# Causal attention with soft expert slots: the upper half of k moved by a transfer within SBUF, the cast of q moved to the pair's second round, and two mask products per score tile in place of three

## The chip, the cores and the metric

The kernel runs on one core of one Trainium2 chip. The metric is the device time of one execution in microseconds (us). Engines are named as the profile names them: PE is the matrix engine (TensorE), PEld its loads of stationary weights, DVE the vector engine, ACT the scalar engine, POOL GpSimd, SP the engine that issues most transfers.

## The reference

The work is causal attention for 8 batches of 12 heads (sequence 448, head size 64), followed by a soft mixture of experts over the attention's output.

```python
scores = scale * np.matmul(q, k.transpose(0, 1, 3, 2))
scores = np.where(mask, -1000000000.0, scores)      # mask: strictly upper triangle
scores = scores - np.max(scores, axis=-1, keepdims=True)
attn = np.exp(scores)
attn = attn / (np.sum(attn, axis=-1, keepdims=True) + 1e-09)
attn_out = np.matmul(attn, v)                       # then x: (3584, 768)
logits = x @ phi                                    # 32 slots, 8 experts
slot_input = softmax(logits, axis=0).T @ x
slot_out[e] = relu(slot_input[e] @ w1[e]) @ w2[e]
out = softmax(logits, axis=1) @ slot_out
```

Everything is float32 from outside.

## The kernel before

**Attention.** Heads go in pairs (`NPAIR` = 48), a pair is loaded together, and each head has one round of the main loop (`for i in range(NHD + 1)`, line 480). Rounds with even `i` (the pair's first head) follow `ORDER[0]`, odd ones `ORDER[1]` (lines 42 to 47). Each tuple is written out by hand and names steps in the order in which every engine gets them; `_InOrder` keeps that order on each engine. Inside round `i` three heads are in work: the first score pass of head `i+2`, the second pass and the exponential of head `i`, and the product with v of head `i-1`.

**Score tile.** A head's causal scores, transposed (keys on partitions), lie in one PSUM tile of 1024 columns (two banks of 512, three such tiles). The four key chunks of 128 start at columns `SCOL` = (512, 0, 320, 960): chunk 0 with its 448 queries and chunk 3 with its 64 fill one bank, chunks 1 and 2 the other. The first pass, `scores1` (line 211), is named `c0`, `c3`, `c12` (mask products: identity in bf16 as weights, the triangle tile `tri` streamed, 128, 64 and 2 x 128 columns) and `k0` to `k3` (weights: a chunk of the rounded k, `ks`; streamed: the rounded q, `qd`; 448, 320, 192 and 64 columns). The second pass, `scores2` (line 285, `t0` to `t3`), adds what rounding left over and the row maximum, with weights `k2` and streamed tile `r2`.

**Operands.** For pair `p`, ACT casts k (`ck`, line 191) and q (`cq`, line 187) to the rounded type. POOL subtracts to get the remainders (`sk`, line 195; `sq`, line 205). ACT copies the rounded k from partitions 0 to 63 of `ks` to partitions 64 to 127 of `k2` (`c2`, `copy_k2`, line 200). Each of these tiles has two buffers, chosen by `p % 2`. In before, `ck` and `cq` of pair `p+2` are both in the even round, `c2` of pair `p+1` at the end of the odd round.

**Row maximum.** ACT evacuates chunk 0's scores (`ev`), DVE takes maxima over the chunks, transposes and reduces (`x0` to `x4`), PE transposes (`mr0`), DVE reduces (`mr1`), POOL spreads the result into `r2` (`sp`). `exp` (ACT) reads the whole score tile, and only after it is that tile free for another head. `a0` to `a3` are the products with v, `n0` to `n2` the normalization. `plan` (line 407) adds, in some rounds, transposes of the result, logits and dispatch; its pattern repeats every 12 rounds.

**Loads.** SP issues all loads: per pair k, v and q, and a tile of expert weights every other pair (22 during attention). A program order on SP, as on the other engines, is the order of the text: the loads stand at the start of odd rounds.

**Start and end.** Scores of heads 0 to 3 are computed ahead of, or in, the first two rounds by `scores1_all`; the steps of these rounds that start with `c`+digit, `k` or `t` and the steps `ev` and `exp` are skipped there. After the attention come the last logits, the experts and the combination, with the remaining expert weights streamed from HBM.

Of the kernel before, what the change touches and what calls it, by code (L numbers as in the profile page):

```python
# [9 lines left out]
F32 = mybir.dt.float32  # L10
F32R = mybir.dt.float32r
BF16 = mybir.dt.bfloat16
AF = mybir.ActivationFunctionType
ALU = mybir.AluOpType
# [3 lines left out]
P = 128  # L18
NB, NH, S, HD = 8, 12, 448, 64
# [10 lines left out]
NEG = -float(2 ** 33)  # L30
NHD = 2 * NPAIR
NR, XB = 2, 3
# [7 lines left out]


ORDER = (
# [4 lines left out]
)  # L47

SC0, SC1, SC2, SC3 = 512, 0, 320, 960
CQ0 = (0, 128, 256, 384)  # L50
SCOL = (SC0, SC1, SC2, SC3)

# [27 lines left out]
def attention_soft_moe(ctx: ExitStack, tc: tile.TileContext, qk, va, phi, w1, w2, out):  # L80
    nc = _Core(tc)
    const = ctx.enter_context(tc.tile_pool(name="const", bufs=1, side="left"))
# [29 lines left out]
    def load_qk(p, a, hs=slice(0, 2)):  # L112
        if p < NPAIR:
            if hs.start == 0:

                st["raw", a, p] = (wres.tile([P, WN], F32, tag="w", name=f"qk{a}_{p}")[:, 0:2 * S]
                                   .rearrange("p (h s) -> p h s", h=2)
                                   if (p, a) in ((1, 0), (2, 1)) else
                                   raw.tile([P, 2, S], F32, tag="qk", name=f"qk{a}_{p}"))
            nc.sync.dma_start(out=st["raw", a, p][:, hs], in_=qk[p, :, a, hs])  # L120

    def loads_v(p, eng=nc.sync):
        if p < NPAIR:
            eng.dma_start(out=va_[p % 2], in_=va[p])
# [12 lines left out]
    def load_w(n):  # L137
        if n < len(order):
            m, e, h, u = order[n]
            t = wtiles[order[n]] = slot(n, f"w{n}")  # L140
            nc.sync.dma_start(out=t, in_=(w1 if m == 0 else w2)[e, h, :, WN * u:WN * u + WN])

    for hs in (slice(0, 1), slice(1, 2)):
# [10 lines left out]
    nc.gpsimd.memset(ident, 0.0)  # L154
    nc.gpsimd.affine_select(out=ident, in_=ident, compare_op=ALU.not_equal, fill=1.0,
                            base=0, pattern=[[-1, P]], channel_multiplier=1)
    tri = const.tile([P, P], BF16, name="tri")
    nc.gpsimd.memset(tri, 0.0)
    nc.gpsimd.affine_select(out=tri, in_=tri, compare_op=ALU.is_ge, fill=NEG,
                            base=0, pattern=[[1, P]], channel_multiplier=-1)  # L160

    ops = [[fix.tile([P, 2, S], F32R, name=f"{o}{i}") for o in ("qd", "ks")] for i in range(NR)]
    qd_, ks_ = ([t[k] for t in ops] for k in range(2))
    ops = [[fix.tile([P, 2, S], F32R, name=f"{o}{i}") for o in ("k2", "r2")] for i in range(NR)]
    k2_, r2_ = ([t[k] for t in ops] for k in range(2))
# [33 lines left out]

    def copy_k2(p, hs=slice(0, 2)):  # L200
        if p < NPAIR:
            nc.scalar.activation(out=k2_[p % NR][64:P, hs], in_=ks_[p % NR][0:64, hs],
                                 func=AF.Copy)

    def sub_q(p, hs=slice(0, 2), eng=None):
        if p < NPAIR:
# [4 lines left out]
    def scores1(i, part):  # L211
        if i >= NHD:
            return
        p, h = divmod(i, 2)
        ks, qd = ks_[p % NR], qd_[p % NR]
        if ("s", i) not in st:
            st["s", i] = ps_s.tile([P, 1024], F32, tag="s", name=f"s{i}")
            st["open"] = set()
        s = st["s", i]

        bank = part in ("c12", "k1", "k2")
        start = bank not in st["open"]
        st["open"].add(bank)
        if part[0] == "k":
            c = int(part[1])
            w, m = S - CQ0[c], min(P, S - P * c)
            nc.tensor.matmul(s[0:m, SCOL[c]:SCOL[c] + w], ks[:, h, P * c:P * c + m],
                             qd[:, h, CQ0[c]:S], start=start, stop=False, skip_group_check=True)
            return
        if part == "c12":  # L230
            o = s[:, SC1:SC1 + 2 * SC2].rearrange("p (a n) -> p a n", n=SC2)[:, :, 0:P]
            mask = tri.unsqueeze(1).to_broadcast([P, 2, P])
        else:
            w = P if part == "c0" else S - 3 * P
            o, mask = s[:, SCOL[int(part[1])]:SCOL[int(part[1])] + w], tri[:, 0:w]
        nc.tensor.matmul(o, identb, mask, start=start, stop=False, skip_group_check=True)

    def scores1_all(i):
        for part in ("c0", "k3", "c3", "c12", "k2", "k1", "k0"):
            scores1(i, part)  # L240

    def max_evac(i):
# [42 lines left out]
    def scores2(i, cs):  # L285
        if i >= NHD:
            return
        p, h = divmod(i, 2)
        s = st["s", i]
        k2, r2 = k2_[p % NR], r2_[p % NR]  # L290
        for c in cs:
            w, m = S - CQ0[c], min(P, S - P * c)
            nc.tensor.matmul(s[0:m, SCOL[c]:SCOL[c] + w], k2[:, h, P * c:P * c + m],
                             r2[:, h, CQ0[c]:S], start=False, stop=True, skip_group_check=True)
# [5 lines left out]
    def attv(i, qcs, first):  # L300
        if not 0 <= i < NHD:
            return
        p, h = divmod(i, 2)
        pt, v, po = pt_[i % 2], va_[p % 2], st.get(("po", i), po0)
        for qc in qcs:
            for c in range(qc + 1):
                col = SCOL[c] + P * (qc - c)


                m = P if qc < 3 or i == NHD - 1 and c < 3 else 65  # L310
                nc.tensor.matmul(po[0:m, qc], pt[:, col:col + m], v[:, c, h],
                                 start=c == 0 and qc in first, stop=c == qc, skip_group_check=True)

# [93 lines left out]
    plan = {}  # L407
    for b in range(NB):
        o, last = 12 * b, b == NB - 1
# [14 lines left out]
    for hs in (h0, h1):  # L424
        cast_k(0, hs)
        cast_q(0, hs)
        sub_k(0, hs, nc.vector)
        sub_q(0, hs)
    scores1_all(0)
    scores1_all(1)  # L430
    warm(START[1])
# [48 lines left out]
    for i in range(NHD + 1):  # L480
        p, h = divmod(i, 2)
        if h:
            load_qk(p + 3, 1)
            if p + 1 < NPAIR - 1:
                loads_v(p + 1)
            load_qk(p + 3, 0)
            if p % 2 and nload < RES:
                load_w(nload)
                nload += 1
        if i == NHD - 3:  # L490

            loads_v(NPAIR - 1, nc.scalar)
        if i < 2:
            scores2(i, (1, 0, 2))
            if i:
                scores1_all(3)
                max_evac(3)
            scores2(i, (3,))
            exps(i)
            if i == 0:  # L500
                max_row(1, 0)
                max_row(1, 1)
                max_spread(1)
                sub_q(1, h1)

        qs = [int(n[1]) for n in ORDER[h] if n[0] == "a"]
        first = qs[:2] if qs[0] == 3 else qs[:1]
        for n in ORDER[h]:
            if i < 2 and (n in ("ev", "exp") or n[0] in "kt" or n in ("c0", "c3", "c12")):
                continue  # L510
            if i == 0 and n in ("mr0", "mr1", "sp"):
                continue
            if n[0] == "k" or n in ("c0", "c3", "c12"):
                scores1(i + 2, n)
            elif n[0] == "t":
                scores2(i, (int(n[1]),))
            elif n[0] == "a":
                attv(i - 1, (int(n[1]),), first)
            elif n[0] == "x":
                max_keys(i + 2, int(n[1]))  # L520
            elif n[0] == "n":
                norm(i - 1, int(n[1]))
            elif n in ("mr0", "mr1"):
                max_row(i + 1, int(n[2]))
            elif n == "ld":
                if i % 12 == 3 and i > 12:
                    logits_d(i // 12 - 1, lt)
            elif n == "plan":
                if later and i:
                    later.pop(0)()  # L530
                plan.get(i, int)()
            else:
                {"ev": lambda: max_evac(i + 2), "exp": lambda: exps(i), "sp": lambda: max_spread(i + 1),
                 "ck": lambda: cast_k(p + 2), "sk": lambda: sub_k(p + 2), "cq": lambda: cast_q(p + 2),
                 "c2": lambda: copy_k2(p + 1), "sq": lambda: sub_q(p + 2)}[n]()
        if i == NHD - 1:

            scs.close()
            pe = att.enter_context(tc.tile_pool(name="pe", bufs=1, space=PSUM, reuse_waits="tile"))
            ps = [pe.tile([P, 512], F32, name=f"e{k}") for k in range(6)]  # L540
            po = st["po", i] = ps[2][:, 0:NCH * VC].rearrange("p (c n) -> p c n", n=VC)
# [44 lines left out]
    for hf in range(2):  # L586
        tps = (po0 if hf == 0 else po).rearrange("p a b->p (a b)")[:, 0:3 * NSLOT]
        for c in range(3):
            o = 384 * hf + P * c
# [130 lines left out]
    n = NBUF  # L720
# [80 lines left out]
```

## Time and profile before

| what | value |
|---|---|
| three runs | 461.1, 459.82, 461.09 us (median 461.09) |
| profiled execution: time / span of its instructions | 459.88 us / 458.2 us |
| busy share of the span: PE, PEld, DVE, ACT, POOL | 93%, 79%, 76%, 72%, 58% |
| mean granted PE clock | 0.978 |
| bytes moved, mean rate | 119.04 MB, 260 GB/s |

All instructions of the kernel body are recorded under one line (line 64, the `_InOrder` helper), so groups are told apart by the tiles that they write and read: `s<-tri,identb` is a mask product, `s<-qd,ks` a first-pass product, `s<-r,k` a second-pass one, `po<-va,pt` the product with v. In this kernel a float32 product (`po`) takes two instructions. A matmul's start is a record, its end is modelled; rows of the timeline that show "x10" cover ten instructions, from the first start to the last end. "128*64 128x192" means weights of 128 rows by 64 columns and 192 streamed columns.

### The profile page before, as it was taken

How to read it: one execution, taken by the hardware profiler on the slowest of the kernel's cores; microseconds unless marked ns; L12 is line 12 of the kernel's file. 1: busy time of each engine (PE TensorE's matmuls, PEld its weight loads, DVE VectorE, ACT ScalarE, POOL GpSimd, SP SyncE). 2: the span in 40 equal slices, each digit the busy share in tenths (PEclk: the TensorE clock that was granted, in tenths of full speed). 3: DMA queues.
4: the chain of work that ended last, by engine and by line, in shares of the span. 5: the costliest groups of instructions: out<-in, count | busy, mean ns of one | idle time of the engine just before them, and what ended most of it. 6: DMA issues, size and time to landing. Idle time of an engine off the chain costs nothing.

```text
span 458.2 us, 12014 instructions
## 1 busy us (share of the span) xinstructions
PE 424.9 (93%) x4581; PEld 362.3 (79%) x4581; DVE 348.9 (76%) x1044; ACT 329.9 (72%) x496; POOL 266.3 (58%) x215
## 2 busy tenths in 40 slices
PE   6899999999999999999999999999999998996660
PEld 3798999999899989998999999999989654542230
DVE  6988888888888898888888888888886467332350
ACT  6898899889888988897899789988975211342240
POOL 5888777777777777777778777777771000000000
PEclk9999999999999999999999999999999999999875
DMA  7477666676667765777666766667758999999997
GB/s 267 128 259 243 235 193 224 216 239 223 204 208 237 236 221 171 241 241 231 210 188 225 254 222 216 191 213 253 231 160 300 369 411 415 414 414 413 402 391 284
DMA packets 38201, 119.04 MB, mean 260 GB/s; under 512 B 4096, under 2 KB 11776, under 8 KB 38144
## 3 DMA queue, kind: packets, MB, share of 16 engines
q1 hardware_dynamic: 38000, 118.01, 75.6%
q8 instruction: 36, 0.59, 0.5%
q10 hardware_dynamic: 144, 0.27, 0.2%
q14 instruction: 21, 0.17, 0.1%
HBM read 107.25 MB, written 11.01 MB: 258 GB/s over the span
## 4 chain that ended last, share of the span: by engine, by line
PE 77%; DMA 11%; POOL 5%; ACT 1%; DVE 1%; issue 1%; SPq 0%; POOLq 0%; ACTq 0%
PE po L64 34%; PE s L64 24%; DMA w<-in_w_dram 10%; PE xt L64 4%; PE g L64 3%; PE hp L64 3%; POOL r L64 3%; PE sp L64 2%; PE rt L64 2%; PE pp L64 2%; POOL ks L64 1%; PE e L64 1%; PE so L64 1%; DMA qk<-in_qk_dram 1%; ACT ot L64 0%
## 5 line engine op out<-in xcount | busy, mean ns | idle before, releaser
L64 PE MATMUL po<-va,pt 128*128 128x65 f32 x1900 | 193.6, 250 | 0.1
L64 PEld LDWEIGHTS po<-va,pt 128*128 128x128 f32 x1900 | 190.5, 171 | 0.5 <-issue 0.3
L64 DVE TENSOR_TENSOR mx<-s,mx 128x320 f32<-128x320 f32 (+2 forms) x288 | 100.8, 350 | 31.4 <-ACT mx L64 27.9
L64 POOL TENSOR_TENSOR r<-qk,qd 64x896 fp32r<-64x896 f32 (+1 forms) x50 | 101.5, 2030 | 6.5 <-ACT qd L64 2.7
L64 POOL TENSOR_SCALAR_AFFINE_SELECT r<-mr 14x448 fp32r<-14x448 f32 x96 | 61.4, 640 | 73.2 <-DVE mr L64 72.8
L64 ACT ACTIVATE pt<-s 128x1024 f32<-128x1024 f32 x96 | 98.2, 1023 | 6.3 <-PE s L64 3.1
L64 POOL TENSOR_TENSOR ks<-qk,ks 64x896 fp32r<-64x896 f32 (+1 forms) x47 | 98.1, 2087 | 4.5 <-ACT ks L64 0.9
L64 PE MATMUL s<-r,k 128*128 128x320 f32 (+3 forms) x384 | 83.2, 298 | 2.3 <-POOL r L64 2.2
L64 ACT ACTIVATE mx<-s 128x448 f32<-128x448 f32 x96 | 52.5, 546 | 36.0 <-PE s L64 22.2
L64 PE MATMUL s<-qd,ks 128*128 128x448 f32 (+3 forms) x384 | 76.0, 308 | 1.6 <-ACT qd L64 1.6
L64 PEld LDWEIGHTS s<-r,k 128*128 128x128 f32 (+1 forms) x384 | 60.0, 176 | 6.4 <-POOL r L64 2.9
L64 DVE STREAM_TRANSPOSE mt<-mx 128x448 f32<-128x448 f32 x96 | 61.9, 645 | 3.3
L64 DVE TENSOR_REDUCE r<-mt 128x14 f32<-128x448 f32 x96 | 58.4, 609 | 0.1
L64 PEld LDWEIGHTS s<-qd,ks 128*128 128x128 f32 (+1 forms) x384 | 55.0, 180 | 3.1 <-ACT qd L64 2.3
L64 ACT ACTIVATE ks<-qk 128x896 fp32r<-128x896 f32 (+1 forms) x50 | 45.6, 914 | 2.5 <-DMA qk<-in_qk_dram 2.5
L64 ACT ACTIVATE k<-ks 64x896 fp32r<-64x896 f32 (+1 forms) x49 | 45.8, 935 | 1.1
L64 ACT ACTIVATE qd<-qk 128x896 fp32r<-128x896 f32 (+1 forms) x50 | 46.1, 923 | 0.4 <-DMA qk<-in_qk_dram 0.3
L64 PEld LDWEIGHTS <-identb 128*128 128x128 bf16 x320 | 28.1, 99 | 20.1 <-issue 15.8
L64 DVE TENSOR_TENSOR x<-po,sm 128x256 f32<-128x256 f32 x95 | 40.3, 424 | 3.3
L64 PE MATMUL s<-tri,identb 128*128 128x64 bf16 (+2 forms) x288 | 39.7, 234 | 0.2
L64 ACT ACTIVATE xts<-xt 128x512 f32<-128x512 f32 x47 | 28.1, 598 | 6.7 <-PE xt L64 4.4
L64 PE MATMUL so<-w,ht 128*32 128x384 f32 x256 | 24.9, 492 | 7.4 <-DMA w<-in_w_dram 5.6
(124 smaller groups left out, 396.2 us busy)
## 6 DMA issues: line engine op xcount, KB each, us to landing
w<-in_w_dram SPq DMA_DIRECT2D x64, 768.0 KB, 7.5
qk<-in_qk_dram SPq DMA_DIRECT2D x94, 448.0 KB, 3.5
va<-in_va_dram SPq DMA_DIRECT2D x47, 260.0 KB, 3.5
out_dram<-ot SPq DMA_DIRECT2D x28, 384.0 KB, 6.5
qk<-in_qk_dram SPq DMA_DIRECT2D x4, 224.0 KB, 3.3
va<-in_va_dram ACTq DMA_DIRECT2D x1, 260.0 KB, 5.4
phi<-in_phi_dram SPq DMA_DIRECT2D x2, 48.0 KB, 3.9
```

Of the source, the lines that this page charges most:

```text
L64: return self._tc.keep_in_program_order(op(*args, **kwargs))
```

## The change

- The three mask products of a head become two: `c03` covers the 64 columns of chunk 3 and the first 128 of chunk 0 in one product (the chunks are moved in the bank so that these 192 columns are adjacent, and the triangle tile is made 192 wide), `c12` is as before. Both stand in a row ahead of `k3`; before, `k3` stood between `c0` and `c12`.
- `copy_k2` becomes a transfer issued by SP, for all pairs but the first, and stands at the start of the even round (the step `c2`) in place of the end of the odd round.
- `cq` moves from the end of the even round to the odd round, behind `exp`.
- The last head's fourth query chunk starts with key chunk 1, and only that one has 128 columns of weights; the others have 65.

```diff
 ORDER = (
-    ("c3", "c0", "k3", "c12", "k1", "k0", "k2", "t0", "t2", "ev", "x1", "t1", "a0", "a3", "t3", "ck",
-     "mr0", "exp", "x0", "a2", "mr1", "x2", "x3", "a1", "cq", "sp", "n0", "sk", "n1", "ld", "n2", "x4", "plan"),
-    ("c3", "c0", "k3", "c12", "k0", "k1", "k2", "ev", "t0", "t1", "t2", "a0", "x0", "t3", "a3", "exp", "mr0",
-     "x1", "mr1", "x2", "x3", "sp", "a2", "a1", "n0", "ld", "n1", "n2", "sq", "c2", "x4", "plan"),
+    ("c2", "c03", "c12", "k3", "k1", "k0", "k2", "t0", "t2", "ev", "x1", "t1", "a0", "a3", "t3", "ck",
+     "mr0", "exp", "x0", "a2", "mr1", "x2", "x3", "a1", "sp", "n0", "sk", "n1", "ld", "n2", "x4", "plan"),
+    ("c03", "c12", "k3", "k0", "k1", "k2", "ev", "t0", "t1", "t2", "a0", "x0", "t3", "a3", "exp", "cq",
+     "mr0", "x1", "mr1", "x2", "x3", "sp", "a2", "a1", "n0", "ld", "n1", "n2", "sq", "x4", "plan"),
 )
-SC0, SC1, SC2, SC3 = 512, 0, 320, 960
+SC0, SC1, SC2, SC3 = 576, 0, 320, 512
...
-    tri = const.tile([P, P], BF16, name="tri")
-    nc.gpsimd.memset(tri, 0.0)
-    nc.gpsimd.affine_select(out=tri, in_=tri, compare_op=ALU.is_ge, fill=NEG,
-                            base=0, pattern=[[1, P]], channel_multiplier=-1)
+    tri3 = const.tile([P, 64 + P], BF16, name="tri")
+    tri = tri3[:, 64:64 + P]
+    nc.gpsimd.memset(tri3, 0.0)
+    for t, n in ((tri3[:, 0:64], 64), (tri, P)):
+        nc.gpsimd.affine_select(out=t, in_=t, compare_op=ALU.is_ge, fill=NEG,
+                                base=0, pattern=[[1, n]], channel_multiplier=-1)
...
-            nc.scalar.activation(out=k2_[p % NR][64:P, hs], in_=ks_[p % NR][0:64, hs],
-                                 func=AF.Copy)
+            if p < 1:
+                nc.scalar.activation(out=k2_[p % NR][64:P, hs], in_=ks_[p % NR][0:64, hs],
+                                     func=AF.Copy)
+            else:
+                nc.sync.dma_start(out=k2_[p % NR][64:P, hs].bitcast(F32),
+                                  in_=ks_[p % NR][0:64, hs].bitcast(F32))
...
-            w = P if part == "c0" else S - 3 * P
-            o, mask = s[:, SCOL[int(part[1])]:SCOL[int(part[1])] + w], tri[:, 0:w]
+            o, mask = s[:, SC3:SC3 + 64 + P], tri3
...
-        for part in ("c0", "k3", "c3", "c12", "k2", "k1", "k0"):
+        for part in ("c03", "k3", "c12", "k2", "k1", "k0"):
...
-            for c in range(qc + 1):
+            last = qc == 3 and i == NHD - 1
+            for c in (1, 0, 2, 3) if last else range(qc + 1):
...
-                m = P if qc < 3 or i == NHD - 1 and c < 3 else 65
+                m = P if qc < 3 or last and c == 1 else 65
```

More of the change, by code (lines that the diff above doesn't have):

```diff
@@ L508, in attention_soft_moe @@
         for n in ORDER[h]:
-            if i < 2 and (n in ("ev", "exp") or n[0] in "kt" or n in ("c0", "c3", "c12")):
+            if i < 2 and (n in ("ev", "exp") or n[0] in "kt" or n in ("c03", "c12")):
                 continue
@@ L512, in attention_soft_moe @@
                 continue
-            if n[0] == "k" or n in ("c0", "c3", "c12"):
+            if n[0] == "k" or n in ("c03", "c12"):
                 scores1(i + 2, n)
```

## The prediction

> **What bounds the kernel now.** I read the page's head first, then the busy times by stretch, then the chain of waits within the attention stretch, then single instructions. The first fence shows the span, PE's busy time and two stretches (columns: length, then PE, PEld, DVE, ACT and POOL busy, PE clock, DMA share, GB/s).
>
> ```profile
> span 458.2 us, 12014 instructions
> PE 424.9 (93%) x4581; PEld 362.3 (79%) x4581; DVE 348.9 (76%) x1044; ACT 329.9 (72%) x496; POOL 266.3 (58%) x215
> ...
> 40.00:342.00 302.00, 302.00 (x3310) 281.85 (x3309) 264.24 (x802) 264.38 (x377) 231.12 (x171) 1.00 0.70 219
> 368.00:458.00 90.00, 64.15 (x697) 31.88 (x689) 37.69 (x104) 22.84 (x57) 0.00 (x0) 0.89 1.00 393
> ```
>
> From 40 to 342 us PE is busy for all of the 302 us, at full clock; ACT has 37.6 us to spare there. The last 90 us have the transfers at 100%, so they only shift. The chain of waits says the same: two rounds of it hold nothing but PE work, round after round.
>
> ```profile
> 204.37 1.17 PE s L64 x10
> 205.54 0.64 PE po L64 x10
> ...
> 207.39 0.78 PE sp L64 x8
> 208.17 1.26 PE s L64 x10
> ...
> 209.62 0.03 PE s L64
> ```
>
> So an edit in this stretch counts by what it does to PE's sequence; ACT time counts only where PE waits for ACT.
>
> **The mask products, the term that decides.** Busy time misleads, since records overlap; what counts is when a product begins. The next rows are one even round's start (start, length, engine, tiles, weights, streamed columns).
>
> ```profile
> 204.10 0.27 PE L64 MATMUL xt<-ident,x 128*128 128x128 f32 x1
> 204.21 0.25 PE L64 MATMUL s<-tri,identb 128*128 128x64 bf16 x2
> 204.27 0.22 PE L64 MATMUL s<-qd,ks 128*64 128x64 f32 x1
> 204.33 0.28 PE L64 MATMUL s<-tri,identb 128*128 128x256 bf16 x1
> 204.37 0.39 PE L64 MATMUL s<-qd,ks 128*128 128x320 f32 x1
> 204.46 0.19 PEld L64 LDWEIGHTS s<-qd,ks 128*128 128x128 f32 x1
> 204.89 0.39 PE L64 MATMUL s<-r,k 128*128 128x448 f32 x1
> ```
>
> The two small masks and `k3` are recorded within 0.06 us of each other, and `k1` (320 columns) only 0.04 us after the 256-column mask, less than that mask needs (0.11 us, below). A matmul's record thus starts before the product does. A weight load's does not: as the rows at 364.18 below show, the weights of one product are loaded while one other streams, and not earlier, so a load starts when the product before its own begins. The load at 204.46, the second one of 128 columns, therefore marks the true start of `k1`. From the first mask to there: 204.46 - 204.21 = 0.25 us. These rows give the prices of the parts:
>
> ```profile
> 360.50 0.83 PE L64 MATMUL po<-tri,identb 128*128 128x256 bf16 x6
> 15.96 0.19 PE L64 MATMUL s<-r,k 128*64 128x64 f32 x1
> 16.07 0.19 PEld L64 LDWEIGHTS po<-va,pt 128*128 128x128 f32 x1
> 364.18 0.85 PE L64 MATMUL po<-sidw,si 128*128 128x32 f32 x6
> 364.18 0.74 PEld L64 LDWEIGHTS po<-sidw,si 128*128 128x128 f32 x6 [0.79 <-DVE si L64]
> ```
>
> - Six masks of 256 columns with the same weights: (0.83 - 0.28)/5 = 0.11 us each, or 0.43 ns a column. So `c03` with 192 columns takes 0.082 us, `c12` 0.11 us; the identity's load hides under either.
> - Six products that stream only 32 columns with new 128-column float32 weights: their loads start (0.74 - 0.19)/5 = 0.11 us apart. The stream is short, and the next load, which can't start before it, sets the pace.
> - The second and third row are the case in question: a product of 64 weight columns and 64 streamed ones (`t3`, once followed by v products in the start phase) at 15.96, and the load that marks the next product's start at 16.07: 0.11 us for a product whose stream is worth 0.03.
>
> Before, `k3` is followed by a mask, whose bf16 identity loads fast (recorded 0.06 us later), and it is the long mask `c12` (0.11 us) under which the wide key weights are loaded. After, `c12` precedes `k3`: it hides only `k3`'s own load, and the 128-column load for `k1` (even) or `k0` (odd) has the 0.03 us of `k3` to hide under. After: 0.082 + 0.11 + 0.11 = 0.302 us, against 0.25, so 0.05; the rows are rounded to 0.01, and I take **0.055 us more in each round**, odd rounds having the same order up to there. Streamed columns are 448 + 64 in both, so nothing is won there; one product less saves 0.082 against 0.43 x (64 + 128) ns = 0.082, nothing. The load can also wait for the end of `k3`'s stream, 0.03 more; or the saving can be an issue slot. Bounds: -0.03 to +0.085 a round. Heads 4 to 95 go this way, 92 rounds: 92 x 0.055 = **+5.1 us**, bounds -2.8 and +7.8. I take 5.1, because the row at 16.07 is the same sequence.
>
> [...]
>
> **k's upper half by transfer.** ACT loses 47 copies.
>
> ```profile
> L64 ACT ACTIVATE k<-ks 64x896 fp32r<-64x896 f32 x47 | 44.7, 950 | 1.1
> w<-in_w_dram SPq DMA_DIRECT2D x64, 768.0 KB, 7.5
> qk<-in_qk_dram SPq DMA_DIRECT2D x94, 448.0 KB, 3.5
> qk<-in_qk_dram SPq DMA_DIRECT2D x4, 224.0 KB, 3.3
> 209.72 0.33 SPq L64 DMA_DIRECT2D qk<-in_qk_dram  x1
> 210.10 0.43 SPq L64 DMA_DIRECT2D w<-in_w_dram  x1
> ```
>
> They become transfers of 224 KB, 10.8 MB on top of 119. On SP the new issue follows the odd round's q and weight loads, issued at 209.72 and 210.10, so it goes out near 210.6; what it needs (`t3` of that round, the piece at 209.62 in the chain; the cast of k, earlier) is done. Its reader is the second pass of the round that begins at 219.22 (below), behind `k3` at 219.28. That leaves over 8.5 us against 3.3 for 224 KB alone, or 7.5 + 3.3 = 10.8 if it queued wholly behind the weight tile's own 7.5; since 7.5 is mostly a median of the saturated last stretch, I count 0. Bounds: 0 to 1.5 us in each of 22 pairs with a weight load, if that queueing were true. Loads of k behind it on SP are issued a round later. On ACT the 0.95 us is off PE's path: 0, and its cover is PE's own round.
>
> **cast of q in the odd round.** It takes the place of the copy right behind `exp`, at the same length (950 against 953 ns), so ACT's odd round is as full as before. But its reader is nearer: `k3` of the next round.
>
> ```profile
> 217.30 1.02 ACT L64 ACTIVATE pt<-s 128x1024 f32<-128x1024 f32 x1
> 218.35 0.95 ACT L64 ACTIVATE k<-ks 64x896 fp32r<-64x896 f32 x1
> 219.22 0.25 PE L64 MATMUL s<-tri,identb 128*128 128x64 bf16 x2
> 219.28 0.22 PE L64 MATMUL s<-qd,ks 128*64 128x64 f32 x1
> ```
>
> The copy ends at 219.30, so a cast there ends at 219.30, too late for a `k3` at 219.28; but the masks now come first. With `exp` 0.055 later, the cast ends at 219.36 and is seen at 219.41 (0.05 us from ACT's end to PE, next fence). The first mask is at 219.275, `k3` begins 0.19 later at 219.47, its weights are wanted 0.06 before that, 219.41: **a tie**, 0. Queued behind a late `k3` is all of PE. Bounds: 0 to 0.1 us in each of 46 pairs, so 0 to 4.6 us. POOL's subtraction of q waits for the same cast and starts some 0.3 us later than now, with POOL 77% busy: 0.
>
> What the emptier even round gives: once in 12 rounds PE waits for ACT before its first mask, since `exp` must free the score tile.
>
> ```profile
> 199.65 1.03 ACT L64 ACTIVATE pt<-s 128x1024 f32<-128x1024 f32 x1
> 200.51 0.27 PE L64 MATMUL tp<-ident,lt 128*128 128x128 f32 x1
> 200.73 0.19 PE L64 MATMUL s<-tri,identb 128*128 128x64 bf16 x1
> ```
>
> `exp` ends at 200.68 and the mask follows 0.05 later, 0.22 after the transpose where 0.11 is usual (204.10 to 204.21). ACT's work from the round before up to this `exp` is unchanged (a cast for a copy), while PE's round grows by 0.055: the wait shrinks by that, 7 times: **-0.4 us**, bounds -0.8 and 0.
>
> **Start and end.** In the first rounds the moved cast is not a tie:
>
> ```profile
> 14.66 0.94 ACT L64 ACTIVATE qd<-qk 128x896 fp32r<-128x896 f32 x1
> 17.69 0.95 ACT L64 ACTIVATE k<-ks 64x896 fp32r<-64x896 f32 x1
> 18.00 0.24 PE L64 MATMUL s<-qd,ks 128*64 128x64 f32 x1
> 18.79 0.70 PE L64 MATMUL s<-r,k 128*128 128x448 f32 x3
> ```
>
> Pair 2's cast now runs at 14.66; in the copy's place it ends near 18.64, and `k3`, now at 18.00, starts at 18.69. From there the three wide products need about 0.55 us, so the second pass starts at 19.24 in place of 18.79. Some of it is caught up where PE has gaps before 40 us (it is busy there 33 of 40 us): **+0.35**, bounds 0 and 0.65. The wider triangle costs POOL one more select at the start, ahead of warm-up products only: 0. In the last head four v instructions shrink from 128 to 65 weight columns:
>
> ```profile
> 202.10 0.66 PE L64 MATMUL po<-va,pt 128*65 128x65 f32 x8
> 202.71 1.23 PE L64 MATMUL po<-va,pt 128*128 128x65 f32 x10
> ```
>
> (1.23 - 0.27)/9 - (0.66 - 0.22)/7 = 0.107 - 0.063 = 0.044 each: **-0.2 us**, bounds -0.2 and 0.
>
> **Sum.** 5.1 - 0.4 + 0.35 - 0.2 = +4.85 us. The profiled execution took 459.88 us for its span of 458.2, so 464.7; against the median of 461.09 (two of three runs lie there, the third is like the profiled one) 465.9. I take **465.7**.
>
> **Rivals.**
>
> - *The key load is prefetched*: `k1`'s load begins under `c12`, two products ahead. Then the mask term is 0 and 0.35 - 0.2 are left, at most 0.4 off for ACT: 460.9 to 461.2. For it: loads do overlap streams. Against: 364.18 and 16.07. Chance 0.12, of which 0.08 no change. [...]
> - *One product less saves an issue slot, the other side.* If each product costs at least the 0.03 us between `c0` and `k3`, one in every head less saves 92 x 0.03 = 2.8 us, and with ACT's wait gone (-0.8) and the end's 0.2: 461.1 - 3.8 + 0.35 = 457.7. It decides where `k1`'s weights come no later than the slot. For it: records 0.03 apart. Against: the phase from 204.21 to 204.89 is 0.68 us for 1472 columns at 0.43 to 0.46 ns, so it streams and has no slot to save. Chance 0.16.
> - *The cast of q becomes the bound* of each pair: the tie goes against PE by 0.1 us, 46 x 0.1 = 4.6 more: 470.3. For it: it ends within 0.01 us of its need. Against: `exp` and masks shift with it. Chance 0.13.
> - *The transfer comes late* in pairs with a weight load: 22 x 0.2 or so, 470. Chance 0.02.
>
> The forecast keeps 0.57. About 0.3% (1.4 us) is what a measurement here can tell from no change. **Faster** 0.18 (the slot, 0.02 of the first rival), **same** 0.09 (the rest of it, and the forecast's lower edge), **slower** 0.73. The likeliest case alone spans 463.5 to 468.0 (0.04 to 0.085 a round, less what the small terms give back). The range reaches to the first rival below and nearly to the late cast above: 459.8 to 469.5.
>
> **What would show it.** Right: between the first mask and the second wide key load 0.30 in place of 0.25 us; rounds without extras some 0.055 longer than now; no row for `k<-ks` on ACT but the first pair's, and PE not waiting for DMA. The wait before 200.73 becomes about half. If `k3` waits for ACT `qd` in every other round, the cast is the bound. If the phase of 0.68 us is 0.65 or less in the new trace, the load was hidden or a slot was saved, and the forecast is wrong.

## The result, and the profile after

The changed kernel takes 465.75 us (median of 6 runs, 464.19 to 467.08) against 461.1 us before (6 runs, 459.66 to 463.04). The ratio is 1.0101, 95% interval 1.0065 to 1.0137: it is slower by 4.65 us. The profiled execution took 464.62 us, its span is 462.9 us, 4.7 more than before.

The page of after, the lines that answer to those shown of before: PE still busy 93%, ACT down from 72% to 63%, the transfers' queue up from 75.6% to 86.5%. The last two lines are the loads of q and k, which now land 4.3 us after their issue (3.5 before), and the new transfer. The queue's line on the page of before comes first.

```profile
q1 hardware_dynamic: 38000, 118.01, 75.6%
```

```profile
span 462.9 us, 11839 instructions
PE 428.5 (93%) x4485; PEld 366.1 (79%) x4485; DVE 349.3 (75%) x1044; ACT 291.2 (63%) x449; POOL 266.2 (58%) x216
...
q1 hardware_dynamic: 41760, 128.79, 86.5%
...
qk<-in_qk_dram SPq DMA_DIRECT2D x94, 448.0 KB, 4.3
...
k<-ks SPq DMA_DIRECT2D x47, 224.0 KB, 6.4
```

The start of an even round of after, as in the prediction (start, length, engine, tiles, weights, streamed columns):

```profile
221.73 0.25 PE L64 MATMUL s<-tri,identb 128*128 128x192 bf16 x1
221.81 0.27 PE L64 MATMUL s<-tri,identb 128*128 128x256 bf16 x1
221.84 0.28 PE L64 MATMUL s<-qd,ks 128*64 128x64 f32 x1
221.92 0.19 PEld L64 LDWEIGHTS s<-qd,ks 128*128 128x128 f32 x1
222.03 0.19 PEld L64 LDWEIGHTS s<-qd,ks 128*128 128x128 f32 x1
222.47 0.39 PE L64 MATMUL s<-r,k 128*128 128x448 f32 x1
```

`c12` is recorded 0.08 us after `c03`. The first wide key load starts at 221.92, which is where `c12`'s stream ends and `k3` begins; the second starts 0.11 later, which is where `k1` begins. From the first mask to there: 222.03 - 221.73 = 0.30 us, 0.25 before. From the first mask to the second pass it is 0.74 us, 0.68 before.

The rounds repeat in a pattern of 12, so the distance of two first masks 12 rounds apart says more than a single round. I compare the same round in every kernel, the one behind the transposes `tp`. Before, and then after:

```profile
200.73 0.19 PE L64 MATMUL s<-tri,identb 128*128 128x64 bf16 x1
244.05 0.19 PE L64 MATMUL s<-tri,identb 128*128 128x64 bf16 x1
```

```profile
202.84 0.27 PE L64 MATMUL tp<-ident,lt 128*128 128x128 f32 x1
202.98 0.24 PE L64 MATMUL s<-tri,identb 128*128 128x192 bf16 x1
246.71 0.24 PE L64 MATMUL s<-tri,identb 128*128 128x192 bf16 x1
```

That is 43.32 us before and 43.73 after, 0.41 more. Counted back from the last head's first mask (345.68 us before, 350.51 after), seven periods of 12 rounds reach to 42.46 and 43.21 us; they start at another round of the pattern than the rows above. Before, all seven take 43.31 to 43.32. After, five take 43.73 to 43.80 and the last two 44.28 and 44.32. These two hold a wait that before doesn't have. The chain of waits of after, at the two places, and PE's waits in the attention stretch:

```profile
272.58 8.29 DMA k<-ks
280.87 0.14 issue
281.01 0.70 PE s L64 x3
...
331.12 8.25 DMA k<-ks
339.37 0.14 issue
339.51 0.71 PE s L64 x3
```

```profile
PE s L64 <- DMA k<-ks: 0.7, 2, 0.4
```

Twice the transfer of k's upper half took over 8.2 us, and the second pass, which would have begun some 0.74 us after its round's first mask, stood until it landed. (The list's 0.7 us counts from the modelled end of the product before; the two periods are 1.1 us longer together.)

So the 4.7 us of the two spans split in four. To the start of the first period after is 0.75 us later. Seven periods at 0.41 are 2.9 us. The seven periods sum to 307.3 us against 303.2, so the two late transfers add 4.1 - 2.9 = 1.2 us. What follows the last head's first mask is 0.1 us shorter.

### The profile page after: what moved, and what is told of

The parts are those of the page before. It is cut to its first block, busy times and chain, and to the rows that moved or that the text cites. A ratio compares the mean times of both kernels' runs of the same rounds, so it can differ in the third digit from the quotient of the medians.

```text
span 462.9 us, 11839 instructions
## 1 busy us (share of the span) xinstructions
PE 428.5 (93%) x4485; PEld 366.1 (79%) x4485; DVE 349.3 (75%) x1044; ACT 291.2 (63%) x449; POOL 266.2 (58%) x216
## 3 DMA queue, kind: packets, MB, share of 16 engines
q1 hardware_dynamic: 41760, 128.79, 86.5%
## 4 chain that ended last, share of the span: by engine, by line
PE 74%; DMA 14%; DVE 3%; POOL 2%; ACT 2%; issue 1%; SPq 0%; POOLq 0%; ACTq 0%
PE po L64 32%; PE s L64 23%; DMA w<-in_w_dram 10%; PE xt L64 4%; DMA k<-ks 4%; PE hp L64 3%; PE g L64 3%; PE sp L64 2%; PE rt L64 2%; PE pp L64 2%; POOL r L64 1%; PE e L64 1%; PE so L64 1%; DVE mx L64 1%; DMA qk<-in_qk_dram 1%
## 5 line engine op out<-in xcount | busy, mean ns | idle before, releaser
L64 PE MATMUL s<-tri,identb 128*128 128x192 bf16 x192 | 34.9, 262 | 0.4 <-ACT pt L64 0.2
L64 PEld LDWEIGHTS <-identb 128*128 128x128 bf16 x224 | 19.0, 100 | 20.1 <-issue 16.5
L64 PE MATMUL xt<-ident,x 128*128 128x128 f32 x188 | 28.5, 274 | 0.0
```

Of the source, the lines that this page charges most:

```text
L64: return self._tc.keep_in_program_order(op(*args, **kwargs))
```

## The experiments

The kernels named here were timed in groups, each group beside the kernel before (medians 460.79, 461.19 and 460.94 us in the three groups).

**Masks alone, in a row (m_row) and with k3 between them (m_between).** Copy on ACT, cast of q in the even round, as before; the masks' columns and the last head's v products as in after.

```diff
-    ("c3", "c0", "k3", "c12", "k1", ...
+    ("c03", "c12", "k3", "k1", ...        # m_row; the odd tuple likewise
+    ("c03", "k3", "c12", "k1", ...        # m_between
```

> Before with the mask products alone changed: c03 and c12 in a row ahead of k3 (and the last head's shorter v products); the cast of q and the ACT copy of k stay where they were. Theory A (a short k3 cannot hide the 0.11 us load of the next 128-column key weights): from the first mask to the second wide key load 0.30 us in place of 0.25, 92 x 0.055 = 5.1 us more, a little of it given back where PE waited for ACT: 465.5 us against 461.1. Rival B (loads are fetched two ahead): no change, 461. Rival C (a product saved is an issue slot of 0.03 us): 458.

> As m_row, but k3 between c03 and c12. Theory A: k3's load hides under c03 (0.08), the wide load under c12 (0.11), so the phase is 0.08 + 0.03 + 0.11 = 0.22 us against 0.25 before: 2 to 3 us faster than before, about 458.5, and 7 us faster than m_row. Rival B: equal to m_row. Rival C: equal to m_row, both 458.

m_row: 465.01 us, ratio 1.0083 (1.0058 to 1.0109). m_between: 460.4 us, ratio 0.9973 (0.9949 to 0.9997). The two have the same products and differ in the place of `k3` alone; the masks in a row cost 4.6 us. The period of 12, first of m_row, then of m_between:

```profile
204.16 0.24 PE L64 MATMUL s<-tri,identb 128*128 128x192 bf16 x1
248.09 0.24 PE L64 MATMUL s<-tri,identb 128*128 128x192 bf16 x1
```

```profile
201.35 0.24 PE L64 MATMUL s<-tri,identb 128*128 128x192 bf16 x1
244.59 0.24 PE L64 MATMUL s<-tri,identb 128*128 128x192 bf16 x1
```

43.93 and 43.24 us, against 43.32: 0.61 more, or 0.05 a round, and 0.08 less. The theory of the key load stands: if a load were fetched two products ahead, or if a saved issue slot decided, the two kernels would be equal. But I expected m_between at 458.5, with 0.22 us from the first mask to the second wide load. It has 0.24:

```profile
219.84 0.25 PE L64 MATMUL s<-tri,identb 128*128 128x192 bf16 x1
219.87 0.25 PE L64 MATMUL s<-qd,ks 128*64 128x64 f32 x1
219.96 0.29 PE L64 MATMUL s<-tri,identb 128*128 128x256 bf16 x1
219.96 0.32 PEld L64 LDWEIGHTS s<-qd,ks 128*128 128x128 f32 x2
```

The mask behind `k3` comes after 0.12 us, as reckoned (0.08 and 0.03). Then the two loads take 0.32 us from the first's start to the second's end, and one is 0.19 long, so they start 0.13 apart, not 0.11. Before has the same spacing: its first wide load is the next row, its second begins at 204.46.

```profile
204.33 0.20 PEld L64 LDWEIGHTS s<-qd,ks 128*128 128x128 f32 x1
```

From one wide load to the next it takes 0.02 us longer under the long mask than behind `k3`; why, these runs don't show. So one product less in itself is worth next to nothing: 0.08 us in 12 rounds.

**The transfer alone (k2_transfer).** Before with this one edit, issued at the start of the even round:

```diff
-            nc.scalar.activation(out=k2_[p % NR][64:P, hs], in_=ks_[p % NR][0:64, hs], func=AF.Copy)
+            if p < 1: ...   # as before
+            else:
+                nc.sync.dma_start(out=k2_[p % NR][64:P, hs].bitcast(F32), in_=ks_[p % NR][0:64, hs].bitcast(F32))
```

> Before with the copy of k's upper half alone turned into the transfer (issued at the start of the even round); masks and cast of q as before. If the ACT copy costs PE time only in the one round of 12 with the softmax statistics (the second pass waits 0.16 us for the copy, the next first mask 0.11 us for exp): 7 x 0.27 = 1.9 us faster, and late transfers give back 0.5 us each for 2 or more of the pairs with a weight load: 459 to 461. If the copy costs nothing anywhere: 461.1 or above, by what the transfers come late.

464.0 us, ratio 1.0047 (1.0016 to 1.0078), above the 459 to 461 of the first branch. The number would fit the second (461.1 or above), but not its reason, that the copy costs nothing. Its shortest periods of 12 are 43.10 us, 0.22 less than before: the ACT copy does have a price. Its other periods reach 44.32. Waits of its attention stretch:

```profile
ACT qd L64 <- DMA qk<-in_qk_dram: 11.1, 18, 1.1
ACT ks L64 <- DMA qk<-in_qk_dram: 2.5, 3, 1.1
PE s L64 <- DMA k<-ks: 1.5, 2, 0.9
```

I had looked only for transfers that come late. The larger effect is that the loads of q come late, 18 times, and the cast of q keeps all of ACT waiting. The loads of q and k are issued at the same place in the round as before, 2.0 us behind its first mask in the median of both, but land after 4.5 us in place of 3.5. Before has no such wait after 45 us.

**Three edits on after (combo), and the same with the late cast (combo_cast_odd).** Expert weights are issued behind the transfer, `k3` stands between the masks; combo has the cast of q back in the even round, combo_cast_odd leaves it in the odd one.

```diff
-            if p % 2 and nload < RES:            # at the loads of the odd round
-                load_w(nload); nload += 1
...
+            elif n == "c2":                      # start of the even round
+                copy_k2(p + 1)
+                if p and p % 2 == 0 and nload < RES:
+                    load_w(nload); nload += 1
```

> After with three edits: k3 between c03 and c12, the cast of q back in the even round, and the load of expert weights issued behind the transfer of k in place of ahead of it. Theory A with the side terms: masks -2 to -3 us, the ACT waits -1.9, no late transfer, the last head -0.2, start as before: 456.5 against 461.1. If the masks' order is not the cause of the loss: 461 or more. If the transfers are late for another reason than the weight load ahead of them: PE waits for k<-ks remain in the profile.

> combo with the cast of q in the odd round, as in after. If combo's waits come from loads of q that land later with the transfer on the queue, and the later cast covers them: ACT no longer waits for q's load (11.8 us in combo), every period of 12 rounds is 43.2 us (43.2 to 44.0 in combo), 2 us less than combo: 460.8, as before or a little under. If they have another cause: 462.8, and the periods stay uneven.

combo: 462.8 us, ratio 1.0033 (1.0009 to 1.0056), far from the 456.5 expected. It is a number of the branch in which the masks' order isn't the cause, but its shortest period, 43.16 us, shows the masks' part gone. combo_cast_odd: 460.91 us, ratio 0.9996 (0.9974 to 1.0018), as expected. Waits on transfers in the attention stretch, first combo, then combo_cast_odd:

```profile
ACT qd L64 <- DMA qk<-in_qk_dram: 11.8, 20, 1.6
```

```profile
ACT ks L64 <- DMA qk<-in_qk_dram: 2.3, 1, 2.3
```

Neither has a wait for `k<-ks` any more. combo's periods run from 43.16 to 44.01; six of combo_cast_odd's lie between 43.16 and 43.29, and the seventh, with the one late load of k, takes 44.90. So once the transfer is on the queue, the late cast is what covers the loads of q. That rests on the waits and the medians; the two intervals overlap by a little, and the profiled execution of combo was the fastest of its 12, with a span of 459.3 us beside 459.4.

**The cast of q back in the even round (after_cq_even).**

```diff
-     "mr0", "exp", "x0", "a2", "mr1", "x2", "x3", "a1", "sp", ...
+     "mr0", "exp", "x0", "a2", "mr1", "x2", "x3", "a1", "cq", "sp", ...
-     ... "a3", "exp", "cq", "mr0", ...
+     ... "a3", "exp", "mr0", ...
```

> After with the cast of q back at the end of the even round. If the moved cast costs the start 0.5 us (the first k3 of the loop waits for it) and nothing later: 465.1 against 465.75, with the start's offset gone. If it was a tie that PE loses by up to 0.1 us in each pair: up to 4 us faster than after. If the emptier even round is what removed the waits of PE for ACT once in 12 rounds: up to 1.6 us slower than after.

468.47 us, ratio 1.0160 (1.0137 to 1.0184) against after's 1.0101 (1.0065 to 1.0137). None of the three reasons that I gave was it: four of its periods are 43.77 us, as in after, and the loss is in the others (44.01, 44.75, 46.48), with waits as in combo:

```profile
ACT qd L64 <- DMA qk<-in_qk_dram: 8.3, 12, 1.6
ACT ks L64 <- DMA qk<-in_qk_dram: 2.4, 2, 2.0
PE s L64 <- DMA k<-ks: 0.2, 1, 0.2
```

**k3 between the masks in after (after_between).**

```diff
-    ("c2", "c03", "c12", "k3", "k1", ...
+    ("c2", "c03", "k3", "c12", "k1", ...
```

> After with k3 between c03 and c12, all else as in after. Theory A: 0.08 us less a round, 92 x 0.08 = 7.4 us faster than after, 458.4; the transfers of k have 0.3 us less time, so waits for k<-ks may give back up to 2 us. If the late cast of q needs both masks ahead of k3: PE waits for ACT qd at k3 in every even round, 0.05 to 0.1 us x 46, and the gain is 3 to 5 us. Rival B (loads two ahead): no change, 465.7.

463.64 us, ratio 1.0062 (1.0034 to 1.0090), 2 us less than after, with intervals that overlap, and not the 7.4 expected. The periods tell more: five of them take 43.20 to 43.31, 0.5 less than after's, so the masks' part is there. They are as short as m_between's, so the late cast doesn't hold up a `k3` that stands between the masks. The last two take 44.25 and 45.24, with PE waiting 2.0 us for `k<-ks` and ACT 4.3 us for loads of k. With shorter rounds the transfers have less time, and part of the gain seems to go back to them; these waits suggest it, no run tests it alone.

**Expert weights behind the transfer in after (after_w_behind).** The edit of combo alone.

> After with the load of expert weights issued behind the transfer of k in place of ahead of it. If the weight load ahead on the queue makes the transfers late: no PE wait for k<-ks, 1.1 us less than after in the profiled execution, and less scatter between runs. If the late transfers come from the queue's load as a whole: no change.

464.57 us, ratio 1.0079 (1.0050 to 1.0109), 1.2 us below after's median. The transfer lands after 5.1 us (6.4 in after), PE has no wait for it, and all seven periods take 43.73 to 43.79. The intervals of the two ratios overlap, so the gain in time isn't settled; that the wait comes from the weight load ahead on the queue is shown by its absence, and by the transfers one by one. Between 60 and 345 us of after, 20 go out right behind a weight load, as in the next rows, and land after 6.8 us in the median; the 20 others take 5.3. With the weight load behind, the two kinds take 5.0 and 5.1.

```profile
271.40 1.14 SPq L64 DMA_DIRECT2D w<-in_w_dram  x1
272.58 0.47 SPq L64 DMA_DIRECT2D k<-ks  x1
```

The scatter between runs (463.36 to 466.32) is as large as after's, so the late transfers don't seem to be its source.

**The ACT copy ahead of the softmax statistics (between_copy_first).** m_between with `c2` right behind `exp`:

```diff
-     ... "a3", "exp", "mr0", ... "sq", "c2", "x4", "plan"),
+     ... "a3", "exp", "c2", "mr0", ... "sq", "x4", "plan"),
```

> m_between (masks merged, k3 between them, copy of k on ACT, cast of q in the even round) with the ACT copy moved from the end of the odd round to right behind exp, so ahead of the softmax statistics that come once in 12 rounds. If that copy's late end in this one round is its only price on PE's path: the period of 12 rounds falls from 43.25 to about 43.1 us, 1 us less in all, 459.4 against 460.4 for m_between. If the copy's length on ACT matters in every round: no change.

460.44 us, ratio 0.9979 (0.9958 to 0.9999), as m_between, and its periods are 43.23 to 43.27. The theory that only the copy's late end costs has fallen. In m_between the second pass once in 12 rounds waits 0.1 us longer than usual, and the next first mask comes 0.21 us after `tp`; here the second pass never waits, and that mask comes 0.38 us after `tp`. The wait has only moved, from the copy's reader to `exp`'s: what counts, it seems, is the whole work of ACT in the two rounds, and the copy is 0.95 us of it.

**The transfer twice (after_double).**

```diff
+                for _ in range(2):
+                    nc.sync.dma_start(out=k2_..., in_=ks_...)
```

> After with the transfer of k issued twice (the same bytes to the same place): 10.8 MB more in the attention stretch. If the transfer's price is time on a queue that is busy 84% there with it: the share goes to about 95%, loads land later still, PE waits for k<-ks and ACT for q's and k's loads in many periods: 5 to 20 us slower than after. If the transfer costs only its own latency: the second one behind the first lands some 1 us later, 2 to 4 us slower.

565.91 us, ratio 1.2261 (1.2210 to 1.2312): a hundred microseconds, and not by the cause that I meant to double. SP's own waits say why:

```profile
SPq L64 <- DMA k<-ks: 294.1, 48, 8.5
```

SP stands until a transfer of k has landed, up to 8.5 us, with every later load behind it. My guess is that the second transfer stands because it writes where the first does; no run tests it. PE's granted clock fell too, to 0.90 between 42 and 446 us against 1.00 in after's attention stretch, so a part of the hundred microseconds may be the clock's. This run doesn't price the transfer's bytes.

## Why the prediction was right, point by point

**The mask products.** The step "0.082 + 0.11 + 0.11 = 0.302 us, against 0.25" is what after's rows show (0.30), and m_row prices it alone. In the seven periods the prediction has 84 x 0.055 - 0.4 = 4.2 us, the mask term with the shrinking wait; m_row's seven take 0.6 more each, 4.2 us. But the wait that shrinks in m_row isn't the one that I read. From `tp` to the mask, where PE waits for `exp`, it is 0.21 us as before (0.22). It is one round earlier that the second pass starts 0.78 us after its round's first mask in both kernels, held by ACT's copy (next point), while elsewhere it starts after 0.68 to 0.70 us in before and 0.74 to 0.76 in m_row. So 11 of 12 rounds pay the 0.055. These rows of m_row answer to 197.24 and 198.02 below:

```profile
200.67 0.35 PE L64 MATMUL s<-tri,identb 128*128 128x192 bf16 x2
201.45 0.44 PE L64 MATMUL s<-r,k 128*128 128x448 f32 x1
```

In these runs the load of key weights starts under the product just ahead of its own, and no earlier: m_row and m_between differ by 4.6 us, and after's two wide loads start 0.11 us apart.

**The ACT time of the copy.** "On ACT the 0.95 us is off PE's path: 0" was wrong, by nearly 0.2 us a period: m_row and after have the masks in the same order, and their undisturbed periods are 43.89 to 43.93 and 43.73 to 43.80. That the copy is the cause, and not the moved cast, k2_transfer shows, where the copy alone is gone and the period falls by 0.22. In the round with the softmax statistics the copy stood behind them. ACT and PE of before there:

```profile
196.24 0.39 ACT L64 ACTIVATE gs<-lt,run_m 128x128 f32<-128x128 f32 x1
196.92 0.95 ACT L64 ACTIVATE k<-ks 64x896 fp32r<-64x896 f32 x1
197.24 0.25 PE L64 MATMUL s<-tri,identb 128*128 128x64 bf16 x2
198.02 0.44 PE L64 MATMUL s<-r,k 128*128 128x448 f32 x1
```

The copy ends at 197.87, and the second pass, which follows its round's first mask (197.24) by 0.68 to 0.70 us elsewhere, is recorded 0.78 after it. I had read the wait for `exp` one round on (0.22 us between `tp` and the mask) and overlooked this one. Both nearly go in after (0.14 us between `tp` and the mask, 0.11 being usual). The seven periods take 307.4 us in m_row and 306.2 in after_w_behind, which has no late transfer: 1.2 us in the change's favour that I hadn't reckoned.

**The transfer.** I counted 0, bounds 0 to 1.5 us in each of 22 pairs. It landed after 6.4 us in the median and 8.3 at most, behind a weight tile, where I had doubted such queueing, and cost after 1.2 us in its profiled execution; "PE not waiting for DMA" failed as a sign. There was also less time than the 8.5 us reckoned: issued at 272.58, the transfer was wanted near 280.54 (279.80, its round's first mask, and 0.74), 8.0 us later. This error and the one before have opposite signs and nearly the same size, and so the sum, 465.7 us, fell on the measured 465.75. That closeness is luck. Of the large terms only the mask term was right by its own working.

**The cast of q.** The tie in the steady rounds held: the shortest periods are 43.73 us in after and 43.77 in after_cq_even, where the cast stands in the even round. But the step has a worth that I had at 0. With the transfer on the queue, the loads of q and k land 0.8 us later, and a cast in the even round waits for them (after_cq_even, combo). The late cast covers that. The prediction has `k3`'s weights wanted 0.06 us ahead of it, which no row shows: in the even round of after shown at the start, the load of `k3` starts at 221.81, 0.11 ahead of `k3`'s start at 221.92, and the cast of q (next rows) has ended at 221.68.

```profile
220.74 0.94 ACT L64 ACTIVATE qd<-qk 128x896 fp32r<-128x896 f32 x1
221.81 0.14 PEld L64 LDWEIGHTS s<-qd,ks 128*64 128x64 f32 x1
```

**Start and end.** 7 x 0.055 + 0.35 = 0.74 us were reckoned ahead of the first period and 0.75 measured. The parts don't agree, though: m_row without the moved cast is 1.3 us later there, and after_cq_even 1.0. The first `exp` begins anywhere from 12.8 us (after) to 14.1 (after_between), 12.9 in before, which moves all that follows. Counted from it, the first period starts after 29.6 us in before, 30.6 in m_row, 30.4 in after and 30.3 in after_cq_even. So the moved cast takes about 0.1 of the 0.35, the masks more than the 0.4 given to them, and why they do is open. The 0.1 us at the end isn't a price of the v products either: m_row has the same end as after, and there it is 0.9 us shorter than before.

**The rivals.** The prefetch and the issue slot fell with m_row and m_between. The late transfer, at a chance of 0.02, is the one that in part came true. The cast of q as a bound of PE didn't.

**What is best.** m_between beats both kernels, before by little: 460.4 us beside 460.79, ratio 0.9973 (0.9949 to 0.9997). It keeps the merged mask, drops the transfer and the moved cast, and puts `k3` back between the masks.

## What to carry to other kernels

On an engine that never pauses (PE of before is busy for all of the 302 us from 40 to 342), look at what each short product hides: a 64-column stream hides only its own 0.03 us of the 0.11 in which the next 128 float32 weight columns are loaded, while a 256-column mask product (0.11 us) hides nearly all of it, so their order is worth more than one product less: 4.6 us between m_row and m_between, against 0.08 us in 12 rounds. Time taken from an engine with slack is still worth something where its work piles up once in many rounds (without ACT's copy, the shortest 12 rounds of k2_transfer take 0.22 us less than before's), and it must be paid for: here a transfer on the shared queue delayed the loads beside it by 0.8 us (after). When a total agrees with a forecast, check the terms; here two errors of more than a microsecond cancelled.

## What the runs showed of the hardware that I had not expected

A 224 KB transfer within SBUF lands after 2.7 us at best and 6.4 us in the median when it shares the queue with the loads (after), and the loads of q and k land after 4.3 us in after and 4.5 in k2_transfer, 3.5 in before. Issued right behind a 768 KB weight tile it takes 6.8 us in the median, otherwise 5.3 (after, 60 to 345 us). From one load of 128 float32 weight columns to the next it is 0.13 us when the first runs under a long bf16 mask (before, m_between), but 0.11 behind a short product (after).
